# Sigmoid attention and a two-layer gated network in one kernel: the second layer's matmuls regrouped by Strassen's seven products

## The chip, the cores and the metric

The kernel runs on one core of a Trainium2 chip. The metric is device time in microseconds (us), the median of several runs: 406.16 us before (406.05 to 406.28 in 3 runs). The engines are PE (TensorE, matmuls; PEld is its weight loading), DVE (VectorE), ACT (ScalarE), POOL (GpSimd) and SP (SyncE). Each runs its own queue of instructions in order; semaphores tie them together. Matmuls write to PSUM, eight banks of 512 float32 columns on 128 partitions; everything else lies in SBUF.

## The reference

```python
scores = scale * np.matmul(q, k.transpose(0, 1, 3, 2)) - np.log(S)
attn = 1.0 / (1.0 + np.exp(-scores))
attn_out = np.matmul(attn, v)              # (8, 12, 448, 64)
x = attn_out.transpose(0, 2, 1, 3).reshape(8 * 448, 12 * 64)
h = x @ w_in                               # (3584, 768) @ (768, 2048)
g = h * (1.0 / (1.0 + np.exp(-beta * h)))
out = g @ w_out                            # (3584, 2048) @ (2048, 768)
```

Inputs and output are float32. The kernel computes its matmuls in float16 with float32 accumulation.

## The kernel before, in words

**Attention.** Eight batches of 12 heads are handled as 24 quads (a quad g is four heads; three quads make a batch b). POOL's queue loads q, k and v and casts them to float16. DVE transposes q and k (L168, L176, L180). A visit of a quad at key tile jt (0 to 3) is 8 matmuls of 32 rows (`score`, L190) into two PSUM tiles `sco` of two banks each; ACT applies the sigmoid to both (`weigh`, L201). The visit at jt = 3, the last 64 keys, takes two quads together every other time. When all four tiles of a quad are weighed, `attend` multiplies them with v (16 matmuls, L256) into two one-bank PSUM tiles, and DVE casts these to `xT` (L265), the transposed input of the dense layers for batch b.

**First layer.** `dense1(b, dc)` is one unit: six matmuls (L276) give 128 of the 2048 hidden columns for the 448 tokens of a batch in a one-bank tile; ACT takes the sigmoid with beta (L284), and DVE multiplies (L287) into `gt`, the hidden values, float16, transposed: 128 partitions x 16 chunks (dc) x 896 tokens. One gt holds a window of two batches, and there are two buffers of it.

**Second layer.** A window has seven tiles of 128 tokens. `dense2(w, t, half, part)` computes one tile's output for one half (384) of the 768 output columns: 16 matmuls (L303) over the hidden chunks, in two parts of eight. The stationary operand is the gt tile, the moving one is `w_out16`. DVE copies the result to `osb` (L316; three buffers of 768 float32 columns), and after the second half SP stores it (L334). For all batches but the last the output rows are interleaved, so a tile goes out in four stores of 32 rows; the last batch goes out with one store a tile. The very last tile is split 512 and 256.

**Order.** The order of each engine is written out by hand (`tc.manual_schedule()`). After a prologue (batch 0, in half widths, while loads come in) a loop goes over 74 visits, numbered 0 to 73 in this document. Behind each visit, units of the dense layers are taken from a list (`filler_stream`): the first layer of a batch, then the tiles that it completes. Each unit has a planned cost (M1_US 1.13, M2_US 2.6 for a half tile, so 1.3 for a part) and the quad from which it may run; a budget, `spread` for the first visits and then `rest` per visit, sets how many. An attend stands ahead of the first visit of the next quad, and DVE's transposes for the next quad behind the second and third. What the loop leaves, the `tail`, runs at the end without visits. PSUM is shared as two `sco` tiles of two banks and four one-bank buffers taken in turn by av, m1 and m2.

Of the kernel before, what the change touches and what calls it, by code (L numbers as in the profile page):

```python
# [13 lines left out]
def kernel(  # L14
# [41 lines left out]
    qTp = ctx.enter_context(tc.tile_pool(name="qTp", bufs=4))  # L56
    kTp = ctx.enter_context(tc.tile_pool(name="kTp", bufs=4))
    attnp = ctx.enter_context(tc.tile_pool(name="attnp", bufs=12))
    xTp = ctx.enter_context(tc.tile_pool(name="xTp", bufs=4))
    gtp = ctx.enter_context(tc.tile_pool(name="gtp", bufs=2))  # L60
    sigp = ctx.enter_context(tc.tile_pool(name="sigp", bufs=3))
    outp = ctx.enter_context(tc.tile_pool(name="outp", bufs=3))
    psum = {}

    def share_psum(pools: ExitStack, n_sc: int, n_one: int):
        for name, bufs in (("sc", n_sc), ("one", n_one)):
            psum[name] = pools.enter_context(
                tc.tile_pool(
                    name=f"ps_{name}{bufs}",
                    bufs=bufs,  # L70
                    space=bass.MemoryType.PSUM,
                    reuse_waits="tile",
                )
            )


    nlogs = const.tile([P, 1], FP32, name="nlogs")
# [167 lines left out]
    def attend(g: int, c0: int, n: int, part=(0, 1)):  # L245
        b, t = divmod(g, QPB)
        if b not in xTs:
            xTs[b] = xTp.tile([P, NHC, S], FP16, tag="xT", name="xT")
        slots = [2 * g + x for x in part]
        avs = [psum["one"].tile([P, S], FP32, tag="one", name="av_ps") for _ in slots]  # L250
        todo = [(s, av, jt) for s, av in zip(slots, avs) for jt in range(JF)]
        for s, av, jt in todo + [(s, av, JF) for s, av in zip(slots, avs)]:
            at = at_tiles.pop((s, jt, c0))
            base, nk = (last_base(s), KL) if jt == JF else (0, P)
            for hh in range(2):
                nc.tensor.matmul(  # L256
                    av[hh * D : (hh + 1) * D, 0:n],
                    vs[b][base : base + nk, 2 * (s % NPAIR) + hh, jt],
                    at[base : base + nk, hh, 0:n],
                    start=(jt == 0),  # L260
                    stop=(jt == JF),
                    tile_position=(base, hh * D),
                )
        for s, av in zip(slots, avs):
            nc.vector.tensor_copy(out=xTs[b][:, s % NPAIR, c0 : c0 + n], in_=av[:, 0:n])  # L265

    gts = {}
    osbs = {}

    def dense1(b: int, dc: int, c0: int = 0, n: int = S):  # L270
        w, off = b // 2, (b % 2) * S + c0
        if w not in gts:
            gts[w] = gtp.tile([P, NDC, WIN], FP16, tag="gt", name="gt")
        m1 = psum["one"].tile([P, S], FP32, tag="one", name="m1_ps")
        for hc in range(NHC):
            nc.tensor.matmul(  # L276
                m1[:, 0:n],
                w_in16[:, hc, dc * P : (dc + 1) * P],
                xTs[b][:, hc, c0 : c0 + n],
                start=(hc == 0),  # L280
                stop=(hc == NHC - 1),
            )
        sg = sigp.tile([P, S], FP32, tag="sg", name="sg")
        nc.scalar.activation(  # L284
            out=sg[:, 0:n], in_=m1[:, 0:n], func=AF.Sigmoid, bias=0.0, scale=beta_sb[:, dc : dc + 1]
        )
        nc.vector.tensor_tensor(  # L287
            out=gts[w][:, dc, off : off + n], in0=m1[:, 0:n], in1=sg[:, 0:n], op=ALU.mult
        )

    m2s = {}
    N2 = 2

    def dense2(w: int, t: int, half: int, part: int):
        gt = gts[w]
        last = w == B // 2 - 1 and t == NTILE - 1
        mid = 512 if last else HALF
        lo, hi = (0, mid) if half == 0 else (mid, DM)
        if part == 0:
            m2s[w, t, half] = psum["one"].tile([P, hi - lo], FP32, tag="one", name="m2_ps")  # L300
        m2 = m2s[w, t, half]
        for dc in range(part * NDC // N2, (part + 1) * NDC // N2):
            nc.tensor.matmul(  # L303
                m2,
                gt[:, dc, t * P : (t + 1) * P],
                w_out16[:, dc, lo:hi],
                start=(dc == 0),
                stop=(dc == NDC - 1),
            )
        if part < N2 - 1:  # L310
            return
        m2s.pop((w, t, half))
        if half == 0:
            osbs[w, t] = outp.tile([P, DM], FP32, tag="osb", name="osb")
        osb = osbs[w, t]
        nc.vector.tensor_copy(out=osb[:, lo:hi], in_=m2)  # L316
        if last:
            store(w, t, lo, hi)
        elif half == 1:
            store(w, t, 0, DM)  # L320

    def store(w: int, t: int, lo: int, hi: int):
        osb = osbs[w, t]
        c, end = t * P, (t + 1) * P
        while c < end:
            b = 2 * w + c // S
            rows, i = out[b * S : (b + 1) * S, lo:hi], c % S
            if b == B - 1:
                n = min(end - c, S - i)
                to = rows[i : i + n]  # L330
# [5 lines left out]

    M1_US, M1H_US, M2_US = 1.13, 0.58, 2.6

    def tiles_after(b: int):
        return range(0, S // P) if b % 2 == 0 else range(S // P, NTILE)  # L340

    def filler_stream():
        for c0 in (0, QH):
            for dc in range(NDC):
                if c0 and dc == 10:
                    for part in range(N2):
                        yield M2_US / N2, 0, lambda part=part: dense2(0, 0, 0, part)
                yield M1H_US, 0, lambda dc=dc, c0=c0: dense1(0, dc, c0, QH)
        for b in range(B):
            if b > 0:  # L350
                for dc in range(NDC):
                    yield M1_US, QPB * (b + 1), lambda b=b, dc=dc: dense1(b, dc)
            todo = [(t, half) for t in tiles_after(b) for half in range(2)]
            for t, half in sorted(todo, key=lambda x: x[1])[1:] if b == 0 else todo:
                for part in range(N2):
                    yield M2_US / N2, 0, lambda a=(b // 2, t, half, part): dense2(*a)

    fill = list(filler_stream())
    at_fill = [0]
# [9 lines left out]
    with tc.manual_schedule():  # L369
# [6 lines left out]
        still = const.tile([P, 512], FP16, name="still")  # L376
        nc.vector.memset(still, 0.0)  # L377
        nc.vector.memset(beta_in, 0.0)
        idle = psum["one"].tile([P, 512], FP32, tag="one", name="idle_ps")

        def idle_units(n: int):
            for _ in range(n):
# [58 lines left out]
        for g in range(QPB + 1, NQUAD, 2):  # L441
            visits += [(g, jt, ()) for jt in range(JF)] + [(g, JF, (g + 1,))]
            visits += [(g + 1, jt, ()) for jt in range(JF)]
        spread = [3 * M1H_US] * 2 + [M2_US, 6 * M1H_US] + [5 * M2_US / 7] * 7

        total = sum(u[0] for u in fill[at_fill[0] :])
        tail = 16 * M1_US + 10 * M2_US
        rest = (total - sum(spread) - tail) / (len(visits) - len(spread))
        budget, spent = 0.0, 0.0
        for i, (g, jt, also) in enumerate(visits):  # L450
            if jt == 0:
                if g > QPB:
                    attend(g - 1, 0, S)
                if g + 2 < NQUAD:
                    if g + 2 not in raws:
# [3 lines left out]
            visit(g, jt, also)  # L459
            if jt in (1, 2) and QPB < g < NQUAD - 1:  # L460
                transpose(g + 1, jt - 1)
            budget += spread[i] if i < len(spread) else rest
            if (g, jt) == (QPB, JF):
                fill_units(3)
# [41 lines left out]
```

## Time and profile before

| | |
|---|---|
| median of 3 runs | 406.16 us |
| the profiled execution | 405.89 us |
| its span, first to last instruction | 404.1 us |
| PE busy | 397.1 us, 98% |
| ACT busy | 236.9 us, 59% |
| DVE busy | 170.1 us, 42% |
| POOL busy | 77.2 us, 19% |
| granted TensorE clock | 1.000 |
| second-layer matmuls (L303) | 896 |
| first-layer matmuls (L276) | 864 |

Times of groups are sums over their instructions; "mean ns of one" counts a matmul from its start to its modelled end, so matmuls in a row overlap, and their pace is read from the time of a run of them. In a group's row the last field is how long the engine had sat idle in front of its instructions, and which engine's work ended that. In the timeline each line is the start, the duration, the engine, the line of the kernel, and the operation with its output and inputs; neighbouring ones are merged ("x8"). The program's PSUM tiles m1_ps and m2_ps appear as m_ps.

### The profile page before, as it was taken

To read this page: it belongs to the slowest core of one execution; us is meant where nothing else is said; L and a number is where in the kernel's file an instruction comes from. 1 tells how busy PE (TensorE), PEld (TensorE's weight loads), DVE (VectorE), ACT (ScalarE), POOL (GpSimd) and SP (SyncE) were. 2 spreads that over 40 slices of the span, in tenths; PEclk is the share of its full clock that TensorE was granted. 3 is DMA by queue.
4 is the path that set the end of the run, shared out by engine and by line. 5 is a ranking of instruction groups with operands and counts; after the bars stand their busy time and mean duration, and the time that the engine had idled before them with its cause. 6 is when DMAs were issued, how large, how long until landed. Compare 5 with 4: busy or idle time off the path is not lost.

```text
span 404.1 us, 7433 instructions
## 1 busy us (share of the span) xinstructions
PE 397.1 (98%) x3087; PEld 200.7 (50%) x3087; DVE 170.1 (42%) x335; ACT 236.9 (59%) x317; POOL 77.2 (19%) x133
## 2 busy tenths in 40 slices
PE   8999999999999999999999999999999999999996
PEld 3467654444554445544455444544445544555563
DVE  2446352355323563354432554245542365225421
ACT  4887856697445784387553786467834677505400
POOL 7833444410141110510114101411100000000000
PEclk9999999999999999999999999999999999999999
DMA  8999999990469212681339302492042200111022
GB/s 120 162 190 203 174 182 202 198 128 5 86 105 136 48 25 56 110 110 34 47 71 170 70 17 47 82 160 47 3 84 50 68 2 0 41 44 36 0 79 78
DMA packets 48801, 35.09 MB, mean 87 GB/s; under 512 B 28272, under 2 KB 45184, under 8 KB 48768
## 3 DMA queue, kind: packets, MB, share of 16 engines
q0 software_dynamic: 43376, 23.60, 44.9%
q1 hardware_dynamic: 5392, 11.02, 9.8%
q8 instruction: 24, 0.39, 0.4%
q14 instruction: 9, 0.07, 0.1%
HBM read 47.19 MB, written 11.01 MB: 144 GB/s over the span
## 4 chain that ended last, share of the span: by engine, by line
PE 88%; DMA 6%; POOL 3%; ACT 2%; issue 0%; DVE 0%; POOLq 0%
PE m_ps L303 36%; PE m_ps L276 35%; PE sco L190 9%; PE av_ps L256 8%; DMA w_in<-in_moe_w_in_dram 4%; ACT attnT L201 2%; DMA v<-in_v_dram 2%; POOL w_in L138 1%; POOL raw L96 1%; POOL v L117 0%; ACT sg L284 0%; DVE osb L316 0%; POOL nlogs L372 0%; POOL dummy L373 0%; POOLq L490 0%
## 5 line engine op out<-in xcount | busy, mean ns | idle before, releaser
L201 ACT ACTIVATE attnT<-sco,nlogs 128x896 f16<-128x896 f32 (+1 forms) x171 | 160.5, 992 | 104.6 <-PE sco L190 104.1
L276 PE MATMUL m_ps<-xT,w_in 128*128 128x448 f16 (+1 forms) x864 | 154.1, 332 | 0.9 <-DMA w_in<-in_moe_w_in_dram 0.7
L303 PE MATMUL m_ps<-w_out,gt 128*128 128x384 f16 (+2 forms) x896 | 153.0, 326 | 0.0
L303 PEld LDWEIGHTS <-gt 128*128 128x128 f16 x896 | 84.5, 98 | 68.0 <-issue 14.8
L287 DVE TENSOR_TENSOR gt<-m_ps,sg 128x448 f16<-128x448 f32 (+1 forms) x144 | 79.9, 572 | 87.4 <-ACT sg L284 87.3
L276 PEld LDWEIGHTS <-w_in 128*128 128x128 f16 x864 | 80.6, 98 | 71.4 <-issue 14.4
L284 ACT ACTIVATE sg<-m_ps,beta_sb 128x448 f32<-128x448 f32 (+1 forms) x144 | 82.4, 596 | 38.1 <-PE m_ps L276 36.4
L316 DVE COPY osb<-m_ps 128x384 f32<-128x384 f32 (+2 forms) x56 | 31.2, 558 | 106.2 <-PE m_ps L303 98.8
L190 PE MATMUL sco<-qT,kT 32*128 32x448 f16 (+3 forms) x864 | 53.0, 340 | 1.4 <-ACT attnT L201 0.8
L96 POOL DMA_DIRECT2D raw<-in_q_dram x27 | 14.9, 553 | 178.6 <-DVE kT L180 175.3
L256 PE MATMUL av_ps<-attnT,v 128*64 128x448 f16 (+3 forms) x432 | 42.2, 340 | 0.3 <-DMA v<-in_v_dram 0.3
L265 DVE CAST xT<-av_ps 128x448 f16<-128x448 f32 (+1 forms) x54 | 28.7, 567 | 30.5 <-PE av_ps L256 30.5
L256 PEld LDWEIGHTS <-v 128*64 128x64 f16 (+1 forms) x432 | 19.0, 107 | 24.8 <-issue 17.6
L190 PEld LDWEIGHTS <-kT 32*128 32x128 f16 (+1 forms) x864 | 13.7, 96 | 30.0 <-issue 27.6
L129 POOL DMA_DIRECT2D v<-in_v_dram x32 | 19.6, 623 | 23.4 <-DMA w_out<-in_moe_w_out_dram 13.4
L117 POOL DMA_DIRECT2D v<-in_v_dram x32 | 19.9, 640 | 7.8 <-DMA w_in<-in_moe_w_in_dram 5.2
L168 DVE STREAM_TRANSPOSE qT<-raw 128x448 f32<-128x448 f32 (+1 forms) x27 | 16.4, 614 | 3.3 <-DMA raw<-in_q_dram 3.3
L176 DVE STREAM_TRANSPOSE kT<-raw 128x384 f32<-128x384 f32 x24 | 13.6, 567 | 2.9 <-DMA raw<-in_k_dram 2.9
L96 POOL DMA_DIRECT2D raw<-in_k_dram x24 | 13.2, 549 | 1.6 <-DMA w_in<-in_moe_w_in_dram 1.6
L383 PE MATMUL idle_ps<-still 128*128 128x512 f16 x31 | 9.5, 451 | 1.2 <-DVE still L377 1.2
L138 POOL DMA_DIRECT2D w_in<-in_moe_w_in_dram x8 | 6.6, 853 | 0.3 <-DMA v<-in_v_dram 0.3
L383 PEld LDWEIGHTS <-still 128*128 128x128 f16 x31 | 3.0, 112 | 5.6 <-issue 3.2
(13 smaller groups left out, 11.8 us busy)
## 6 DMA issues: line engine op xcount, KB each, us to landing
out_dram<-osb SPq DMA_DIRECT2D x98, 96.0 KB, 1.9
raw<-in_k_dram POOLq DMA_DIRECT2D x24, 224.0 KB, 4.9
raw<-in_q_dram POOLq DMA_DIRECT2D x21, 224.0 KB, 3.6
v<-in_v_dram POOLq DMA_DIRECT2D x32, 144.0 KB, 6.9
w_in<-in_moe_w_in_dram POOLq DMA_DIRECT2D x8, 384.0 KB, 11.6
w_out<-in_moe_w_out_dram POOLq DMA_DIRECT2D x4, 768.0 KB, 15.2
v<-in_v_dram POOLq DMA_DIRECT2D x32, 48.0 KB, 5.9
out_dram<-osb SPq DMA_DIRECT2D x2, 384.0 KB, 2.3
```

The source lines that it names most:

```text
L96: nc.gpsimd.dma_start(out=raws[g][:, r, c0:c1].rearrange("p c d -> p (c d)"), in_=(q, k)[r][b, HQ * t : HQ * (t + 1)].rearrange("h (p c) d ...
L117: nc.gpsimd.dma_start(out=vs[b][i * BLK : (i + 1) * BLK, :, 0:JF].rearrange("p h j d -> p h (j d)"), in_=rows[:, :, JF * i * D : JF * (i + ...
L129: nc.gpsimd.dma_start(out=vs[b][lo : lo + BLK, :, JF], in_=rows[:, :, c])
L190: nc.tensor.matmul(sco[base : base + nk, hh, u0 : u0 + n], kT[g][lo : lo + BLK, jt * P : jt * P + nk, e], qT[g][lo : lo + BLK, c0 : c0 + n ...
L201: nc.scalar.activation(out=at[:, :, 0:n], in_=sco[:, :, 0:n], func=AF.Sigmoid, bias=nlogs[:, 0:1], scale=MSCALE,)
L256: nc.tensor.matmul(av[hh * D : (hh + 1) * D, 0:n], vs[b][base : base + nk, 2 * (s % NPAIR) + hh, jt], at[base : base + nk, hh, 0:n], start ...
L265: nc.vector.tensor_copy(out=xTs[b][:, s % NPAIR, c0 : c0 + n], in_=av[:, 0:n])
L276: nc.tensor.matmul(m1[:, 0:n], w_in16[:, hc, dc * P : (dc + 1) * P], xTs[b][:, hc, c0 : c0 + n], start=(hc == 0), stop=(hc == NHC - 1),)
L284: nc.scalar.activation(out=sg[:, 0:n], in_=m1[:, 0:n], func=AF.Sigmoid, bias=0.0, scale=beta_sb[:, dc : dc + 1])
L287: nc.vector.tensor_tensor(out=gts[w][:, dc, off : off + n], in0=m1[:, 0:n], in1=sg[:, 0:n], op=ALU.mult)
L303: nc.tensor.matmul(m2, gt[:, dc, t * P : (t + 1) * P], w_out16[:, dc, lo:hi], start=(dc == 0), stop=(dc == NDC - 1),)
L316: nc.vector.tensor_copy(out=osb[:, lo:hi], in_=m2)
```

## The change

24 of the 28 token tiles are now computed in 12 pairs. The hidden values of tiles t and t+1 are a 2 x 2 block matrix A: rows are the two tiles, columns the two halves of the 2048 hidden columns. `w_out16` is a 2 x 2 block matrix B: rows are halves of the hidden columns, columns the two halves of the 768 output columns. Instead of eight block products of eight matmuls each, a pair has seven. Two of them take a block of A as it is, five a sum or difference of two blocks; DVE makes these with one float16 instruction of 8 x 128 columns each (`hidden_sum`), two products ahead, into three buffers. Five sums of blocks of w_out are made once, by DVE, in ten half instructions behind visits 5 to 13 (`weight_sum`, `adds`).

The products of a pair accumulate in four one-bank PSUM tiles: r takes products 0 and 5, a takes 1, 4 and 6, s takes 2, b takes 3. In between, what r and a hold is read while they stay open, and the outputs of both tiles are put together from them: two copies by ACT and five adds or subtractions by DVE per pair, in place of four DVE copies. The store of tile t+1 follows product 5, that of tile t product 6.

A tile may now hold its bank across other work, so the four banks are taken by hand (`bank`): the one longest unused that is not held. If more than two are held ahead of an attend, which needs two, the loop first takes units until they aren't.

`gt` has one buffer instead of two, `xT` three instead of four. Tiles 0, 1, 2 and 27 go as before. Units of the second layer are four matmuls instead of eight, planned at 0.65 us. The planner spends 2.95 us on each of visits 11 to 31 and `rest` after them; its tail is planned at nine half tiles instead of ten.

```diff
-    xTp = ctx.enter_context(tc.tile_pool(name="xTp", bufs=4))
-    gtp = ctx.enter_context(tc.tile_pool(name="gtp", bufs=2))
+    xTp = ctx.enter_context(tc.tile_pool(name="xTp", bufs=3))
+    sump = ctx.enter_context(tc.tile_pool(name="sump", bufs=3))
...
+    def bank(name: str, cols: int = S, hold=None):
+        i = min((i for i in used if i not in held.values()), key=used.get)
+        used[i] = max(used.values()) + 1
+        if hold is not None:
+            held[hold] = i
+        return psum["one"].tile([P, cols], FP32, tag=f"one{i}", name=name)
...
-        avs = [psum["one"].tile([P, S], FP32, tag="one", name="av_ps") for _ in slots]
+        avs = [bank("av_ps") for _ in slots]
...
+    gt = const.tile([P, NDC, WIN], FP16, name="gt")
...
+    ND = NDC // 2
+    B11, B12, B21, B22 = (
+        w_out16[:, r * ND : (r + 1) * ND, c * HALF : (c + 1) * HALF]
+        for r in range(2)
+        for c in range(2)
+    )
+    ws = {
+        name: const.tile([P, ND, HALF], FP16, name=f"w_{name}")
+        for name in ("T1", "T3", "T4", "T6", "T7")
+    }
+
+    def weight_sum(name: str, part: int):
+        x, y, op = {
+            "T1": (B11, B22, ALU.add),
+            "T3": (B12, B22, ALU.subtract),
+            "T4": (B21, B11, ALU.subtract),
+            "T6": (B11, B12, ALU.add),
+            "T7": (B21, B22, ALU.add),
+        }[name]
+        rows = slice(part * ND // 2, (part + 1) * ND // 2)
+        nc.vector.tensor_tensor(out=ws[name][:, rows], in0=x[:, rows], in1=y[:, rows], op=op)
+
+    def hid(t: int, half: int):
+        return gt[:, half * ND : (half + 1) * ND, cols(t)]
+
+    def product(t: int, i: int):
+        A11, A12, A21, A22 = hid(t, 0), hid(t, 1), hid(t + 1, 0), hid(t + 1, 1)
+        return (
+            ("r", A11, None, None, ws["T3"]),
+            ("a", A22, None, None, ws["T4"]),
+            ("s", A11, A12, ALU.add, B22),
+            ("b", A21, A22, ALU.add, B11),
+            ("a", A11, A22, ALU.add, ws["T1"]),
+            ("r", A21, A11, ALU.subtract, ws["T6"]),
+            ("a", A12, A22, ALU.subtract, ws["T7"]),
+        )[i]
+
+    def hidden_sum(t: int, i: int):
+        _, x, y, op, _ = product(t, i)
+        if op is not None:
+            sums[t, i] = sump.tile([P, ND, P], FP16, tag="sum", name="sum")
+            nc.vector.tensor_tensor(out=sums[t, i], in0=x, in1=y, op=op)
+
+    def strassen(t: int, i: int, part: int):
+        name, x, _, op, w = product(t, i)
+        if part == 0 and i + 2 < NPROD:
+            hidden_sum(t, i + 2)
+        first = (t, name) not in m2s
+        if first:
+            m2s[t, name] = bank("m2_ps", HALF, (t, name))
+        m2 = m2s[t, name]
+        for dc in range(part * ND // 2, (part + 1) * ND // 2):
+            nc.tensor.matmul(
+                m2,
+                (x if op is None else sums[t, i])[:, dc],
+                w[:, dc],
+                start=first and dc == 0,
+                stop=(dc == ND - 1),
+                skip_group_check=i >= 4,
+            )
+            first = False if dc else first
+        if part == 0:
+            return
+        if i == 0:
+            for u in (t, t + 1):
+                osbs[u] = outp.tile([P, DM], FP32, tag="osb", name="osb")
...
+        if i == 1:
+            nc.scalar.copy(out=o2[:, L], in_=a)
+        elif i == 2:
+            nc.scalar.copy(out=o1[:, L], in_=m2)
+            add(o1[:, R], r, o1[:, L])
+            release((t, "s"))
+        elif i == 3:
+            add(o2[:, L], m2, o2[:, L])
+            release((t, "b"))
+        elif i == 4:
+            add(o2[:, R], a, o2[:, L], ALU.subtract)
+        elif i == 5:
+            add(o2[:, R], r, o2[:, R])
+            release((t, "r"))
+            store(t + 1, 0, DM)
+        elif i == 6:
+            add(o1[:, L], a, o1[:, L], ALU.subtract)
+            release((t, "a"))
+            store(t, 0, DM)
...
+    def second_layer(tiles):
+        for t in tiles:
+            if t < 3 or t == NT - 1:
+                for half in range(2):
+                    for part in range(N2):
+                        yield M2_US / N2, lambda a=(t, half, part): dense2(*a)
+            elif t % 2:
+                for i in range(NPROD):
+                    for part in range(2):
+                        yield M2_US / 4, lambda a=(t, i, part): strassen(*a)
...
+        for b in range(1, B):
+            for dc in range(NDC):
+                yield M1_US, QPB * (b + 1), lambda b=b, dc=dc: dense1(b, dc)
+            ends = [((x * S // P) - 1) // 2 * 2 + 1 for x in (b, b + 1)]
+            for cost, unit in second_layer(range(ends[0], NT if b == B - 1 else ends[1])):
+                yield cost, 0, unit
...
+        spread += [2.95] * (sum(g < 4 * QPB for g, _, _ in visits) - len(spread))
...
-        tail = 16 * M1_US + 10 * M2_US
+        tail = 16 * M1_US + 9 * M2_US
...
+        adds = {
+            5: [("T4", 0)],
+            6: [("T4", 1)],
+            8: [("T3", 0)],
+            9: [("T3", 1), ("T1", 0)],
+            10: [("T1", 1), ("T6", 0)],
+            11: [("T6", 1)],
+            12: [("T7", 0)],
+            13: [("T7", 1)],
+        }
...
             if jt == 0:
                 if g > QPB:
+                    while len(held) > 2:
+                        spent += fill[at_fill[0]][0]
+                        fill_units(1)
                     attend(g - 1, 0, S)
...
+            for name, part in adds.get(i, ()):
+                weight_sum(name, part)
```

A pair is named below by its first tile: pairs 3, 5, 7, ... 25. Where two pairs follow each other with no first-layer units between them, these are 3 and 5, 9 and 11, 13 and 15, 17 and 19, and 23 and 25; pairs 23 and 25 and tile 27 are in the tail.

## The prediction

> **What bounds the kernel now.** I first read the page's busy times, then the chain that ended last.
>
> ```profile
> PE 397.1 (98%) x3087; PEld 200.7 (50%) x3087; DVE 170.1 (42%) x335; ACT 236.9 (59%) x317; POOL 77.2 (19%) x133
> ...
> PE m_ps L303 36%; PE m_ps L276 35%; PE sco L190 9%; PE av_ps L256 8%; DMA w_in<-in_moe_w_in_dram 4%; ACT attnT L201 2%; DMA v<-in_v_dram 2%; POOL w_in L138 1%; POOL raw L96 1%; POOL v L117 0%; ACT sg L284 0%; DVE osb L316 0%; POOL nlogs L372 0%; POOL dummy L373 0%; POOLq L490 0%
> ```
>
> TensorE (PE) is the bound. The sums over stretches of 20 us show it busy for 20.00 in every stretch from 80 us to 380 us, so a removed matmul is time saved, and each new wait of PE is time lost, unless it falls in the load phase before 45 us. ScalarE (ACT) and VectorE (DVE) are behind it on the mean, so I next read their forms and an ordinary step of the loop.
>
> ```profile
> L303 PE MATMUL m_ps<-w_out,gt 128*128 128x384 f16 x864 | 147.8, 326 | 0.0
> ...
> L284 ACT ACTIVATE sg<-m_ps,beta_sb 128x448 f32<-128x448 f32 x112 | 69.1, 636 | 34.4 <-PE m_ps L276 34.4
> L287 DVE TENSOR_TENSOR gt<-m_ps,sg 128x448 f16<-128x448 f32 x112 | 68.1, 624 | 74.0 <-ACT sg L284 74.0
> ...
> L284 ACT ACTIVATE sg<-m_ps,beta_sb 128x224 f32<-128x224 f32 x32 | 13.4, 455 | 3.7 <-PE m_ps L276 1.9 <-DVE gt L287 0.4
> ...
> L287 DVE TENSOR_TENSOR gt<-m_ps,sg 128x224 f16<-128x224 f32 x32 | 11.8, 388 | 13.5 <-ACT sg L284 13.4
> ...
> L377 DVE MEMSET still<- 128x256 uint32 x1 | 0.3, 272 | 0.9 <-PEq L490 0.9
> ```
>
> The 326 ns of one matmul overlaps its neighbours; its pace is read from the end of the chain, where 128 of them run alone:
>
> ```profile
> 362.04 18.16 PE m_ps L276 x96
> 380.20 20.81 PE m_ps L303 x128
> ```
>
> 20.81/128 = 0.163 us each; eight are 1.30. A dense1 unit is 18.16/16 = 1.13. The timeline of one step:
>
> ```profile
> 261.30 1.64 PE L256 MATMUL av_ps<-attnT,v 128*64 128x448 f16 x16
> ...
> 262.87 0.57 PE L190 MATMUL sco<-qT,kT 32*128 32x448 f16 x8
> 262.97 1.16 DVE L265 CAST xT<-av_ps 128x448 f16<-128x448 f32 x2 [2.31 <-PE av_ps L256]
> ...
> 263.38 4.07 PE L303 MATMUL m_ps<-w_out,gt 128*128 128x384 f16 x24
> 263.48 1.91 ACT L201 ACTIVATE attnT<-sco,nlogs 128x896 f16<-128x896 f32 x2 [2.87 <-PE sco L190]
> ```
>
> An attend takes PE 1.57 (261.30 to 262.87), a visit's scores 0.51, its two weighings take ACT 1.91, the two casts that free an attend's PSUM banks take DVE 1.16, each hand-over about 0.1. ACT had idled 2.87 us before this weighing, so it has slack in the second layer's stretches.
>
> **What goes.** 24 of 28 tiles had 32 matmuls each, 768. Twelve pairs have 7 x 8 = 56, 672. The 96 that go are 96 x 0.163 = **15.6 us**. Nothing else on PE changes in number.
>
> **What comes.** ACT gets 24 copies of 384 columns: on the line through the two forms of L284, (636-455)/224 = 0.81 ns a column, 455 + 160 x 0.81 = 0.58 us, 14 us in all; ACT goes to 251 of some 390. DVE gets 60 adds with a PSUM input; by L287's forms, 1.05 ns a column, 388 + 160 x 1.05 = 0.56 us, for 48 evictions gone that took 0.56 too (L316's group): +6.7 us. It gets 60 sums of hidden tiles (1024 f16 columns) and ten half weight sums (1536). No row shows a two-input f16 sum in SBUF. L287's line carried on gives 152 + 1024 x 1.05 = 1.23 us and 1.77; that is the upper end. The only all-f16 write in SBUF, the memset of 512 f16, is done as 256 words in 272 ns; if the sum also goes by words, it is 152 + 512 x 1.05 = 0.69 and 0.96, the lower end. I take 0.69, since the two-input rows all read float32 from PSUM, which the sums don't. DVE is then 170 + 6.7 + 41 + 10 = 228 of 390 (with 1.23: 268). On the mean both are covered by idle DVE time.
>
> The Trainium skill ("VectorE: DVE Perf Modes", the perf-mode tier table) has a bf16 tensor_tensor in SBUF at two elements a cycle, 1224 ns for 2048; by its figures I estimate 0.69 for 1024, the case I took. Against the change it says ("SBUF — State Buffer", Who interferes with whom) that a VectorE instruction with two SBUF inputs contends with GpSimd's reads. In the trace before, every two-input instruction of VectorE reads one input from PSUM, so it shows nothing of this; by the rule POOL could lose at most the 51 us of sums, an estimate, and it is idle for 81% of the span.
>
> **Where PE waits anew.** Adding up the planner's costs, I numbered the 74 visits (0 to 73) and the units behind each; a pair spreads over some 2.9 visits. "3.4" is product 4 of pair 3. Four one-bank accumulators serve everything. A pair holds r over products 0 to 5, a over 1 to 6, s over 2 and b over 3, so an attend inside a pair needs the banks of s and b back. s is read by an ACT copy, b by a DVE add, and both queues are in order.
>
> Pairs that follow at once (3 to 5, 9 to 11, 13 to 15, 17 to 19; 23 to 25 in the tail) have one more link: three output buffers, two a pair, so the second pair's tile t+1 takes the buffer of the first pair's tile t. With T the end of the first pair's last product, its add ends at T+0.7. The stores:
>
> ```profile
> L334 SPq DMA_DIRECT2D out_dram<-osb x103: 314/421/1235, 66.5 to 401.5; - x103
> ...
> DMA to landing us min/median/max: 1.7/2.0/6.7
> ```
>
> Four stores of 32 rows go out 0.42 us apart; tile t+1's hold SP until T+1.1, t's go out to T+2.8 and land at T+4.8. The ACT copy of a, ready at T+2.7, stands in ACT's queue until T+4.8, and behind it stands the next visit's weighing.
>
> - Visits 20 to 22: after 3.6 come 5.0, 5.1, scores, 5.2, 5.3, then an attend at T+5.7. ACT: copy of a to T+5.4, weighing to T+7.3, copy of s to T+7.9. So the attend's first bank comes at T+8.0 (2.3 late). Then DVE: add of s 0.56, a hidden sum 0.69, add of b 0.56, to T+10.0. The second bank should have come 0.55 after the first, and comes 1.5 later still. **3.9 us** with hand-overs.
> - Visits 53 and 64 (pairs 15 and 19): the attend comes right behind product 2, at T+4.4; copies of a and s run from T+4.8 to T+6.0; the second accumulator, due T+4.95, waits 1.2; the next product then needs the bank of the first cast, 0.6 + 0.1 after the attend, with scores of 0.5 between: 0.25. **2.9 us** for both.
> - Visits 39 and 50: the same without the store, copy of s 0.7 after product 2, due 0.55: 0.2 + 0.25 each; visit 18: 0.25. **1.15 us.** At visits 29 to 32, 41 to 43, 60 and 71 banks and copies are in time.
> - Weight sums stand in visits 5 to 13 on DVE. Visits 9 and 10 get two each, 1.92 of a step of 2.45 us, with 0.42 of eviction and 0.7 of transposes: 0.6 too much each, and the casts of visit 11, which dense1 needs at once, come later. Ends 0 and 4 (at 1.77); I take **1.0**.
> - Tail: the last multiply of dense1 ends 1.5 behind PE's switch in the trace, so the first sum is ready at 2.2 us and due at 2.6. DVE needs 5 x 0.69 + 5 x 0.56 = 6.3 of a pair's 9.1. Its stores are one per tile, 3.0 behind T, and the copy delayed by them is wanted at T+5.2. **0**, with 1.23 a sum about 1 per pair.
> - One gt and three xT buffers cost nothing: every matmul that reads the old gt columns stands on PE ahead of the dense1 that overwrites them, and an xT is rewritten three batches later. If not, DVE's multiply, then the m1 banks, would be late.
> - Units of four move where a visit stands by at most 0.65 us, no work. Visits with two dense1 units instead of three give PE 0.5 + 2.27 = 2.8 for ACT's 1.91 + 1.27 = 3.2; they alternate with longer ones, so 0.
>
> **Sum.** 404.1 - 15.6 + 3.9 + 2.9 + 1.15 + 1.0 = 397.45 us of span. The profiled execution took 405.89, 1.79 more than its span, and the median is 0.27 above that: 397.45 + 2.06 = **399.5**.
>
> **Rivals.**
> 1. *The waits are covered.* If stores land sooner or ACT is ahead, the crossings cost next to nothing. For: at 254 us four issues start within 1.3 us, and ACT idles 2.87 per step. Against: the in-order queues above. 404.1 - 15.6 + 1.5 + 2.06 = 392.1.
> 2. *VectorE becomes the bound inside the pairs; slower.* At 1.23 a sum, a pair asks 6.15 + 2.8 + 0.8 attends x 1.16 + 0.8 x 1.41 of transposes = 11.0 of DVE, where PE takes 9.1 + 2.9 x 0.51 + 0.8 x 1.57 = 11.8. The add of s waits for a copy that stands behind a weighing, 1.91 + 0.58 = 2.5 of forced idling: 13.5, so +1.7 for ten pairs, 1 for each of two in the tail, 4 at the weight sums: 23 us. 404.1 - 15.6 + 23 + 2.06 = 413.6. It decides from about 0.9 us a sum (8.9 + 2.5 = 11.8 from 5 sums of 0.8 to 0.9 on), and it is slower than before once a pair loses more than 1.5. Against: the f16 memset by words.
> 3. *The copies reload ACT's table.* The one table load of the trace takes 1283 ns. Two at each of 24 copies are 61.6 us of ACT; a pair leaves ACT about 11.8 - 2.9 x 1.91 - 1.2 = 5.1, as much as is needed, but weighings and banks come 2.6 later each time. About 3 us a pair: 399.5 + 30 = 430. For it the trace shows nothing: before, the engine runs one function only.
>
> That the matmuls don't fall in number can't be: the loops count them.
>
> **Chances.** Forecast (395 to 404) 0.56, the first rival 0.26, the second 0.14, the third 0.04. The range reaches down to the first rival with its waits at nothing, 404.1 - 15.6 + 1 + 2.06 = 391.5, and up to 406, the forecast with the weight sums at 4 and the longer sums in the tail (404.5) and a further 1.5 for a store landing later. A measurement of this kernel tells some 0.2% from no change, 0.8 us. Faster 0.83 (both first cases and a little of the second), same 0.04, slower 0.13.
>
> **What would show it.** PE matmuls 2991 and busy some 15 less than before; the sum rows near 0.69 us; PE idle in front of the attends' av_ps, released by ACT copies or DVE adds, above all in visits 21 and 22 (some 130 us in); ACT copies of osb released by out_dram stores. Wrong: a second ACT table load, sums over 1 us, or PE full throughout (then 392).

## The result, and the profile after

The changed kernel takes **393.62 us**, the median of four runs (392.94 to 394.52), against 406.18 (406.05 to 406.28) in the same series: a ratio of 0.9692, 95% interval 0.9673 to 0.9712, or 12.6 us less. The profiled execution took 394.52, the slowest of the four, with a span of 392.7; before, 405.89 and 404.1. An execution of the same kernel profiled later took 393.03, with a span of 391.3. Single executions of one kernel differ by some 2 us: in later series the kernel before lay between 405.43 and 407.22, the changed kernel between 393.03 and 395.58.

The page of the changed kernel, busy time by engine and the chain that ended last:

```profile
PE 382.2 (97%) x2991; PEld 191.9 (49%) x2991; DVE 220.2 (56%) x417; ACT 247.3 (63%) x341; POOL 77.0 (20%) x133
...
PE m_ps L286 36%; PE m_ps L398 27%; PE av_ps L268 9%; PE sco L202 9%; DMA w_out<-in_moe_w_out_dram 4%; PE m_ps L316 3%; DMA w_in<-in_moe_w_in_dram 2%; DMA v<-in_v_dram 2%; POOL raw L108 1%; DMA out_dram<-osb 1%; DVE xT L277 1%; DVE osb L417 1%; POOL v L129 0%; ACT sg L294 0%; DVE gt L297 0%
```

TensorE is still the bound. It has 96 matmuls fewer and is busy 14.9 us less; the span is 11.4 shorter, so about 3.5 us of what was removed came back, nearly all of it as waits (below). VectorE gained 50 us of work, ScalarE 10, GpSimd none.

The operations that are new, in the view of groups by shape (busy, mean ns of one, idle time just before and what ended it):

```profile
L387 DVE TENSOR_TENSOR sum<-gt 128x1024 f16<-128x1024 f16 x60 | 39.2, 679 | 0.1
...
L417 DVE TENSOR_TENSOR osb<-m_ps,osb 128x384 f32<-128x384 f32 x60 | 33.3, 555 | 41.9 <-ACT osb L422 22.5 <-PE m_ps L398 18.5
...
L362 DVE TENSOR_TENSOR w_T<-w_out 128x1536 f16<-128x1536 f16 x10 | 9.1, 928 | 0.0
```

```profile
L422 ACT COPY osb<-m_ps 128x384 f32<-128x384 f32 x12 | 5.8, 480 | 5.8 <-PE m_ps L398 5.8
L420 ACT COPY osb<-m_ps 128x384 f32<-128x384 f32 x12 | 5.7, 478 | 16.4 <-PE m_ps L398 16.4
...
L501 ACT ACT_TABLE_LOAD x1 | 1.3, 1283 | 0.7 <-PEq L633 0.7
```

A hidden sum takes 0.68 us, half a weight sum 0.93, an add 0.56, a copy 0.48, and there is one table load, as before. None of the copies waited for a store: L420's idle time is put down to PE alone.

What PE waited for (line and what it waited for: us in all, times, longest). Before:

```profile
PE idle_ps L383 <- DVE still L377: 1.2, 1, 1.2
PE sco L190 <- ACT attnT L201: 0.8, 3, 0.3
PE m_ps L276 <- DMA w_in<-in_moe_w_in_dram: 0.7, 1, 0.7
```

and after:

```profile
PE m_ps L316 <- DMA w_out<-in_moe_w_out_dram: 1.7, 2, 1.4
PE av_ps L268 <- DVE osb L417: 1.3, 2, 0.7
PE idle_ps L510 <- DVE still L504: 1.2, 1, 1.2
PE m_ps L398 <- DVE xT L277: 1.0, 5, 0.2
PE m_ps L286 <- DVE osb L417: 0.6, 1, 0.6
PE sco L202 <- DVE kT L188: 0.6, 1, 0.6
```

All waits come to 3.5 us before and 7.1 after. Three things are to be seen. The waits in and behind the attends of visits 22, 53 and 64, forecast at 6.8 us, are 1.1: 0.69 at an accumulator (av_ps) in visit 22, and 0.2 each behind the attends of visits 53 and 64. The other half of the 1.3 at av_ps, 0.65, stands in visit 32, where none was forecast. A wait for w_out of 1.7 that wasn't forecast stands at the start of the second layer; the execution profiled later has none, and its waits come to 5.3. And the three waits of the scores for ScalarE (0.8), which the kernel had before, are gone.

The place where most was forecast is the attend in visit 22, inside pair 5, which follows pair 3 at once. The timeline of the changed kernel there (start, duration, instruction, idle time before it), ScalarE's queue first, then VectorE's, then the attend on PE:

```profile
115.86 0.48 ACT L420 COPY osb<-m_ps 128x384 f32<-128x384 f32 x1 [1.45 <-PE m_ps L398]
116.46 1.90 ACT L213 ACTIVATE attnT<-sco,nlogs 128x896 f16<-128x896 f32 x2
118.25 0.48 ACT L422 COPY osb<-m_ps 128x384 f32<-128x384 f32 x1
```

```profile
118.77 0.56 DVE L417 TENSOR_TENSOR osb<-m_ps,osb 128x384 f32<-128x384 f32 x1 [3.14 <-ACT osb L422]
119.24 0.68 DVE L387 TENSOR_TENSOR sum<-gt 128x1024 f16<-128x1024 f16 x1
119.84 0.55 DVE L417 TENSOR_TENSOR osb<-m_ps,osb 128x384 f32<-128x384 f32 x1
```

```profile
119.00 0.76 PE L268 MATMUL av_ps<-attnT,v 128*64 128x448 f16 x6
120.44 1.07 PE L268 MATMUL av_ps<-attnT,v 128*64 128x448 f16 x10 [0.69 <-DVE osb L417]
```

Pair 3 ended (T) at 113.2. The copy of a, forecast to wait for a store until T+4.8, ran at T+2.7, as soon as product 1 was done. The attend's first accumulator was in time; the second came 0.69 late, behind the copy of s (which stood behind a weighing), the add of s, a hidden sum and the add of b.

### The profile page after: what moved, and what is told of

The parts are those of the page before. It is cut to its first block, busy times and chain, and to the rows that moved or that the text cites. A ratio compares the mean times of both kernels' runs of the same rounds, so it can differ in the third digit from the quotient of the medians.

```text
span 392.7 us, 7403 instructions
## 1 busy us (share of the span) xinstructions
PE 382.2 (97%) x2991; PEld 191.9 (49%) x2991; DVE 220.2 (56%) x417; ACT 247.3 (63%) x341; POOL 77.0 (20%) x133
## 4 chain that ended last, share of the span: by engine, by line
PE 84%; DMA 9%; DVE 2%; POOL 2%; issue 1%; ACT 1%; SPq 0%; POOLq 0%
PE m_ps L286 36%; PE m_ps L398 27%; PE av_ps L268 9%; PE sco L202 9%; DMA w_out<-in_moe_w_out_dram 4%; PE m_ps L316 3%; DMA w_in<-in_moe_w_in_dram 2%; DMA v<-in_v_dram 2%; POOL raw L108 1%; DMA out_dram<-osb 1%; DVE xT L277 1%; DVE osb L417 1%; POOL v L129 0%; ACT sg L294 0%; DVE gt L297 0%
## 5 line engine op out<-in xcount | busy, mean ns | idle before, releaser
L398 PEld LDWEIGHTS <-sum 128*128 128x128 f16 x480 | 45.5, 98 | 37.6 <-issue 9.0
L417 DVE TENSOR_TENSOR osb<-m_ps,osb 128x384 f32<-128x384 f32 x60 | 33.3, 555 | 41.9 <-ACT osb L422 22.5
L202 PE MATMUL sco<-qT,kT 32*128 32x448 f16 (+3 forms) x864 | 51.9, 340 | 0.9 <-DVE kT L188 0.6
L398 PE MATMUL m_ps<-w_T,sum 128*128 128x384 f16 x288 | 50.5, 327 | 0.0
L108 POOL DMA_DIRECT2D raw<-in_q_dram x27 | 14.9, 552 | 169.7 <-DVE kT L192 167.0
L387 DVE TENSOR_TENSOR sum<-gt 128x1024 f16<-128x1024 f16 x60 | 39.2, 679 | 0.1
L398 PE MATMUL m_ps<-w_out,sum 128*128 128x384 f16 x192 | 34.2, 326 | 1.0 <-DVE xT L277 1.0
L398 PE MATMUL m_ps<-w_T,gt 128*128 128x384 f16 x192 | 33.7, 327 | 0.0
L398 PEld LDWEIGHTS <-gt 128*128 128x128 f16 x192 | 18.1, 98 | 14.6 <-issue 3.1
L316 PE MATMUL m_ps<-w_out,gt 128*128 128x384 f16 (+2 forms) x128 | 22.7, 327 | 1.7 <-DMA w_out<-in_moe_w_out_dram 1.7
```

What stands on the lines that cost most here:

```text
L202: nc.tensor.matmul(sco[base : base + nk, hh, u0 : u0 + n], kT[g][lo : lo + BLK, jt * P : jt * P + nk, e], qT[g][lo : lo + BLK, c0 : c0 + n ...
L316: nc.tensor.matmul(m2, gt[:, dc, cols(t)], w_out16[:, dc, lo:hi], start=(dc == 0), stop=(dc == NDC - 1),)
L387: nc.vector.tensor_tensor(out=sums[t, i], in0=x, in1=y, op=op)
L398: nc.tensor.matmul(m2, (x if op is None else sums[t, i])[:, dc], w[:, dc], start=first and dc == 0, stop=(dc == ND - 1), skip_group_check= ...
L417: nc.vector.tensor_tensor(out=out, in0=in0, in1=in1, op=op)
```

## The experiments

**Theory A**, formed from that timeline: the forecast wait is a real mechanism that the changed kernel misses, because of the buffer that the pool hands out. Tile 4's store is issued ahead of tile 3's and lands first (three of its four parts after 1.8 to 1.9 us, the last after 4.2; tile 3's took 5.5 to 6.3). Tile 6, which is written first (the copy of a), gets the third buffer, long free; tile 5, written next (the copy of s), gets tile 4's. The addresses in the built program show the order: by first writing the tiles go 0, 1, 2, 4, 3, 6, 5, 8, 7 and so on, and along this row the three buffers take turns. The prediction counted the turns by tile number and so gave tile 6 tile 3's buffer. What waits remain come from the order in which banks and adds follow. **Theory B**: the buffers don't matter, since the stores are early enough anyway, and the cost is elsewhere: the sums on VectorE, or the rate of the planned fill at the start.

### The changed kernel again

> The changed kernel as it is, as the measure of the other runs on this chip. Both theories expect 393.6 (its four earlier runs lay between 392.9 and 394.5).

Measured 393.24 us (393.03 to 395.58), ratio 0.9696 [0.9676, 0.9715]. It stood beside the next three on one chip.

### Buffers in turn by tile number

```diff
-    outp = ctx.enter_context(tc.tile_pool(name="outp", bufs=3))
+    outp = ctx.enter_context(tc.tile_pool(name="outp", bufs=1))
...
-            osbs[t] = outp.tile([P, DM], FP32, tag="osb", name="osb")
+            osbs[t] = outp.tile([P, DM], FP32, tag=f"osb{t % 3}", name="osb")
...
-                osbs[u] = outp.tile([P, DM], FP32, tag="osb", name="osb")
+                osbs[u] = outp.tile([P, DM], FP32, tag=f"osb{u % 3}", name="osb")
```

> Output buffers are given to tiles in turn (tile number modulo 3), as the prediction assumed, instead of in the order in which they come free. Theory A: the prediction's chain of waits was right and only its buffer assignment was not, so tile 6 of pair 5 now waits for the store of tile 3, ACT's copy of a holds the next weighing and the copy of s, and PE idles in front of the attends in pairs 5, 15 and 19: 4 to 7 us more than the changed kernel, 398 to 401. Theory B: ACT has enough slack in these stretches to swallow a late copy: within 0.5 us of the changed kernel.

Measured **406.81 us** (405.84 to 408.61, 12 runs), ratio 1.0018 [1.0007, 1.003]: the whole gain is gone, 13.6 us, by which of three buffers a tile is given. ScalarE's waits in this kernel, PE's, and the timeline of ScalarE and PE in visits 20 to 22:

```profile
ACT osb L420 <- DMA out_dram<-osb: 22.5, 4, 9.1
```

```profile
PE av_ps L268 <- ACT osb L422: 8.4, 3, 4.8
```

```profile
121.15 0.48 ACT L420 COPY osb<-m_ps 128x384 f32<-128x384 f32 x1 [6.76 <-DMA out_dram<-osb]
121.52 1.91 ACT L213 ACTIVATE attnT<-sco,nlogs 128x896 f16<-128x896 f32 x2
123.31 0.49 ACT L422 COPY osb<-m_ps 128x384 f32<-128x384 f32 x1
```

```profile
123.85 1.33 PE L268 MATMUL av_ps<-attnT,v 128*64 128x448 f16 x6 [4.81 <-ACT osb L422]
125.51 1.85 PE L268 MATMUL av_ps<-attnT,v 128*64 128x448 f16 x10 [0.33 <-DVE osb L417]
```

It is the chain of the prediction, link by link: the copy of a held by a store, the weighing behind it, the copy of s behind that, and PE in front of the attend's bank. (Only the second bank came 0.33 late, where 1.5 was forecast.) At pairs 15 and 19 it shows again, with waits of 2.5 and 1.1. So theory A holds, and the chain is dearer than either theory had it, for two reasons. The copy waited until T+8.0 instead of T+4.8: in this stretch stores take longer to land (the last section). And PE was slower after the wait. Sums over stretches of this kernel (from:to, length; busy us and instructions of PE, weight loads, DVE, ACT, POOL; granted clock of PE; DMA share; GB/s):

```profile
119.00:125.00 6.00, 1.19 (x7) 0.67 (x7) 1.17 (x3) 2.65 (x4) 0.80 (x2) 0.88 1.31 150
125.00:130.00 5.00, 4.67 (x26) 1.56 (x24) 2.21 (x4) 1.74 (x2) 0.00 (x0) 0.50 0.01 3
130.00:135.00 5.00, 5.00 (x34) 2.56 (x33) 2.22 (x4) 1.88 (x3) 0.00 (x0) 0.96 0.29 67
```

After the wait PE ran at half the clock for about 6 us: the attend's last ten matmuls took 1.85 us and the 20 of the second layer behind them 4.52, against 1.07 and 3.42 in the changed kernel. The two reasons make up nearly all of the difference in span to the profile after, 14.1 us: PE's waits come to 16.2 us here against 7.1 (9.1 more), and PE is busy for 386.8 us with the same 2991 matmuls, against 382.2 (4.6 more).

### A released bank counts as used when it is released

```diff
-        held.pop(key)
+        used[held.pop(key)] = max(used.values()) + 1
```

> A released bank counts as used at its release instead of at its taking. Theory A: of PE's waits in the profile, the two of 0.65 us at 160.7 and 164.9 us come from handing out the bank of r or a right after its last product, while others are long free: 1.3 us less than the changed kernel, 392.3. The waits of 0.2 us for a cast and of 0.7 at 119.8 us stay. Theory B: the wait moves to the next bank in line and nothing is gained: 393.6.

Measured 391.49 us (390.88 to 391.84), ratio 0.964 [0.9628, 0.9653]. A second series gave 392.03, ratio 0.9654 [0.9637, 0.9671]:

> The run with the banks alone once more, as the measure of the other two on this chip: 391.5 by both theories (390.9 to 391.8 before).

What it undoes is seen on PE in the changed kernel's timeline at visit 32:

```profile
157.91 2.76 PE L398 MATMUL m_ps<-w_T,sum 128*128 128x384 f16 x16
161.32 1.64 PE L268 MATMUL av_ps<-attnT,v 128*64 128x448 f16 x16 [0.65 <-DVE osb L417]
162.89 0.57 PE L202 MATMUL sco<-qT,kT 32*128 32x448 f16 x8
163.40 1.47 PE L398 MATMUL m_ps<-w_T,sum 128*128 128x384 f16 x8
165.52 1.67 PE L286 MATMUL m_ps<-xT,w_in 128*128 128x448 f16 x8 [0.65 <-DVE osb L417]
```

`bank` takes the bank that was *taken* longest ago. The banks of r and a were taken at products 0 and 1, so they are handed out the moment products 5 and 6 are done with them, while the closing add still reads them, and other banks have been free for longer. Both waits of 0.65 are gone with the edit. The gain is 1.8 us against the changed kernel beside it, and by the ratios of the second series, (0.9696 - 0.9654) x 406, 1.7 us; the two waits are 1.3 of it, the rest is not placed.

### The fill of the start, later

```diff
-        spread = [3 * M1H_US] * 2 + [M2_US, 6 * M1H_US] + [5 * M2_US / 7] * 7
+        spread = [3 * M1H_US] * 2 + [M2_US, 6 * M1H_US] + [M2_US / 2] * 4 + [M2_US] * 3
```

> The same units of tiles 0 to 2, but 1.3 us of them behind each of visits 4 to 7 and 2.6 behind 8 to 10 instead of 1.86 behind each. Theory A: the two waits of 1.7 us at 61 and 63 us come from the units of four reaching the second half of w_out before it has landed; spent later they go, and the short visits give back about 0.3 us three times: 0.8 us less, 392.8. Theory B: the load phase is bound by its transfers, and PE waits for something else instead: no gain or up to 1 us of loss.

Measured 394.56 us (394.34 to 394.98), ratio 0.9719 [0.9706, 0.9731]: 1.3 us longer than the changed kernel beside it, at the edge of what the runs tell apart (the two intervals overlap). The wait for w_out isn't there, but the changed kernel beside it had none either, and two small new waits came in this stretch (0.22 and 0.28). So that wait is not a fixed cost of the change, and no gain from later units shows. PE's waits come to 6.6 us against 5.3 in the changed kernel's trace beside it; what is left of the 1.3 more, beyond those two, stands in the first 23 us, ahead of anything that the edit touches.

### The change's side parts alone, in the kernel before

Units of four matmuls, one gt buffer, three xT buffers; no pairs.

```diff
-    xTp = ctx.enter_context(tc.tile_pool(name="xTp", bufs=4))
-    gtp = ctx.enter_context(tc.tile_pool(name="gtp", bufs=2))
+    xTp = ctx.enter_context(tc.tile_pool(name="xTp", bufs=3))
+    gtp = ctx.enter_context(tc.tile_pool(name="gtp", bufs=1))
...
-    N2 = 2
+    N2 = 4
```

> The kernel before with the change's side parts alone: units of four matmuls, one gt buffer, three xT buffers; no products of Strassen. Theory A: the buffers cost nothing, since all readers of the old gt columns stand ahead on PE; the units of four remove three waits of 0.28 us for ACT and may bring up to 1.7 us of waiting for w_out: 405.3 to 407. Theory B: one gt buffer makes DVE's multiplies late: over 408.

Measured 404.39 us (403.64 to 405.08), ratio 0.9957 [0.994, 0.9973], 1.5 us less than the kernel before in that series. The three waits of the scores for ScalarE's weighings (0.8 us in the trace before) are gone, and no wait for gt or xT came. The rest of the 1.5 is not placed.

### The hidden sums made twice

```diff
+            nc.vector.tensor_tensor(out=sums[t, i], in0=x, in1=y, op=op)
```

> Each of the 60 hidden sums is issued twice, 0.68 us more of DVE each, 41 in all; a pair then asks 5 x 1.36 of DVE, more than the 1.23 of the prediction's second rival. Theory A: DVE's idle time covers most, and only the adds and casts that free banks ahead of an attend come 0.7 later in some crossings: 394 to 397. Theory B, the rival: DVE bounds the pairs and each loses 1.7 us: 411 or more.

Measured 404.18 us (402.64 to 404.6), ratio 0.9947 [0.993, 0.9965]: 11 us of the gain gone, between what the two theories gave. VectorE is busy 259.6 us of 402.7, 64% on the mean, and yet PE waits for it:

```profile
PE m_ps L399 <- DVE osb L418: 4.3, 5, 1.2
PE av_ps L268 <- DVE osb L418: 3.4, 2, 2.0
```

All waits come to 13.6 us, against 5.3 in the changed kernel's later execution, and PE is busy for 385.2 us with the same matmuls, against 382.3; a stretch at half clock (last section) is part of that. Inside the pairs VectorE is close to full, as this kernel's sums over stretches show, first within pair 3 and then in a stretch of first-layer units (columns as above, VectorE third):

```profile
100.00:110.00 10.00, 9.79 (x76) 4.87 (x73) 9.25 (x17) 5.74 (x8) 1.05 (x2) 1.00 0.30 48
140.00:150.00 10.00, 10.00 (x77) 4.43 (x74) 5.25 (x10) 8.53 (x13) 1.06 (x2) 1.00 0.30 48
```

In 155 to 164 us, up to the longest wait (2.0), it was busy for 8.75 us of 9. So the sums are hidden at their price of 0.68 us, not at 1.36. The idle 36% lies mostly outside the pairs, where it can't help a sum that stands between a bank's last product and the add that frees it. In kind this is the bound of theory B; its cost was put too high.

### The hidden sums left out

The five sums of a pair are not made; the product reads the first block in place of the sum.

```diff
-            sums[t, i] = sump.tile([P, ND, P], FP16, tag="sum", name="sum")
-            nc.vector.tensor_tensor(out=sums[t, i], in0=x, in1=y, op=op)
+            sums[t, i] = x
```

> The 60 hidden sums are left out: a product takes the first of its two blocks as it is, so the output isn't the reference's; matmuls, adds, copies and weight sums stay. Theory A: the sums are covered but for the one between the two adds of pair 5, which holds the attend 0.7 us: 392.4 to 393.2. Theory B: sums delay casts and adds at many crossings: under 391.

Measured 392.92 us (392.41 to 394.43), ratio 0.9688 [0.9667, 0.9709]. Without any sum the kernel is not measurably faster than the changed kernel (393.24). Of PE's waits at DVE's adds only that in pair 5 is gone (0.7 us).

### Copies on VectorE

Both copies of a pair move from ScalarE to VectorE.

```diff
-            nc.scalar.copy(out=o2[:, L], in_=a)
+            nc.vector.tensor_copy(out=o2[:, L], in_=a)
...
-            nc.scalar.copy(out=o1[:, L], in_=m2)
+            nc.vector.tensor_copy(out=o1[:, L], in_=m2)
```

> The two copies of a pair run on DVE instead of ACT. Theory A: the wait of 0.7 us in pair 5 comes from the copy of s standing behind a weighing in ACT's queue; on DVE it goes, and 13 us more of DVE are covered: 392.5 to 393.2. Theory B: DVE's own queue, now with copies between sums, frees the banks of s and b later at the other crossings: 394 to 396.

Measured 393.47 us (392.99 to 393.8), ratio 0.969 [0.9675, 0.9704]: no difference. The wait in pair 5 falls from 0.68 to 0.32. With the released banks added,

> A released bank counts as used at its release, and the two copies of a pair run on DVE. Theory A: the two savings add, 0.35 us under the run with the banks alone: 391.1. Theory B: ACT was not what held the bank: 391.5.

391.53 us (391.04 to 392.93), ratio 0.9646 [0.9624, 0.9668], no different from the released banks alone.

### Sums a product earlier

The released banks, and each sum three products ahead instead of two, with a fourth sum buffer and one sigmoid buffer fewer to make room.

```diff
-    sump = ctx.enter_context(tc.tile_pool(name="sump", bufs=3))
-    sigp = ctx.enter_context(tc.tile_pool(name="sigp", bufs=3))
+    sump = ctx.enter_context(tc.tile_pool(name="sump", bufs=4))
+    sigp = ctx.enter_context(tc.tile_pool(name="sigp", bufs=2))
...
-        if part == 0 and i + 2 < NPROD:
-            hidden_sum(t, i + 2)
+        if part == 0:
+            for j in (2, 3) if i == 0 else (i + 3,):
+                if j < NPROD:
+                    hidden_sum(t, j)
```

> A released bank counts as used at its release, and the hidden sums run three products ahead (four buffers for them, paid for with one of the three sigmoid buffers). Theory A: the last bank wait of 0.7 us, in pair 5, goes, since no sum stands between the two adds any more: 0.7 us under the run with the banks alone (391.5), 390.8. Theory B: two sigmoid buffers make ACT wait for DVE in the first layer's stretches, or the third sum at a pair's start delays DVE elsewhere: 391.5 or more.

Measured 391.23 us (391.15 to 392.91), ratio 0.9647 [0.9625, 0.9669]. The wait in pair 5 stayed, 0.63: product 3 now issued the sum for product 6 exactly between the two adds, so the edit had moved one sum out of the way and another into it. With two sigmoid buffers ScalarE waits 1.6 us for VectorE in all, and the scores once for a weighing, 0.4 us. With no sum issued by product 3:

```diff
-            for j in (2, 3) if i == 0 else (i + 3,):
-                if j < NPROD:
-                    hidden_sum(t, j)
+            for j in {0: (2, 3), 1: (4,), 2: (5,), 4: (6,)}.get(i, ()):
+                hidden_sum(t, j)
```

> As the run with the banks and the sums three ahead, but product 3 issues no sum, so none stands between the adds of s and b. Theory A: the wait of 0.6 to 0.7 us ahead of the attend in pair 5 falls to 0.1 or less, and the span by 0.6; the median, 390.9 to 391.5, can hardly tell it from the run before. Theory B: the wait stays, since the copy of s behind a weighing holds the bank, not the sum.

Measured **390.65 us** (390.43 to 390.95), ratio to the kernel before 0.9613 [0.9599, 0.9627]: the fastest version found, beside 0.9692 for the changed kernel. The timeline of DVE and PE in pair 5 of this version:

```profile
117.49 1.02 DVE L418 TENSOR_TENSOR osb<-m_ps,osb 128x384 f32<-128x384 f32 x2 [2.47 <-ACT osb L423]
119.67 1.16 DVE L277 CAST xT<-av_ps 128x448 f16<-128x448 f32 x2 [1.16 <-PE av_ps L268]
```

```profile
117.78 1.85 PE L268 MATMUL av_ps<-attnT,v 128*64 128x448 f16 x16
```

The two adds follow each other, and the 16 matmuls of the attend run without a break. The wait in pair 5 is gone, as its theory A said. PE's waits come to 3.5 us, as in the kernel before, and the span is 14.9 us shorter; PE is busy 14.8 less (382.3 us against 397.1). This version ran in a series without the released banks alone beside it, so how much of the last step the removed wait brought can't be told from the medians.

## Why the prediction was right, and where it was wrong

It said 399.5 us in a range of 391.5 to 406, and faster. The direction and the range hold; the gain was put at 6.7 us and is 12.6. The stretch that it gave to its own forecast, 395 to 404, was missed: the measured time lies in the part of the range that reaches down to the first rival.

- **What goes.** 15.6 us of matmuls; PE is busy 14.9 less. Right, within 0.7.
- **What comes.** The lower end chosen for a hidden sum, 0.69, measured 0.68; half a weight sum 0.96, 0.93; an add 0.56, the same; a copy 0.58, 0.48. DVE at 220 us, put at 228. The lower end was the right choice, but the memset is weak ground for it: its row shows an instruction on 256 32-bit words, not a sum of f16 tiles, and its 272 ns are less than 152 + 256 x 1.05 = 421. From the two rows measured a sum takes (928 - 679)/512 = 0.49 ns a column. The figure in the Trainium skill ("VectorE: DVE Perf Modes", the perf-mode tier table), two elements a cycle, agrees with the 0.68 measured.
- **GpSimd's share.** Of the rule against the change ("SBUF — State Buffer", Who interferes with whom) no run here shows a cost: POOL is busy 77.0 us against 77.2, with 48 us of two-input SBUF instructions added on VectorE. POOL's rows are issues of loads and a few memsets, none with an input in SBUF, so this is hardly a test of it.
- **The waits behind stores, 6.8 us in visits 20 to 22, 53 and 64: the step that failed.** It reads "three output buffers, two a pair, so the second pair's tile t+1 takes the buffer of the first pair's tile t". The turns don't go by tile number: tile t+1 is written before tile t, so it gets the buffer that is free, and tile t the one of the first pair's tile t+1, whose store was issued first. The waits there were 0.7 and 0.4. Forcing the order that the sentence assumes brings the chain back, and costs 13.6 us; so the mechanism was right, its condition wrong, and its size also wrong, since the late landing and the clock weren't in it. Had the buffers gone by tile number, the forecast would have been too low by 7. That the measured time falls within the range is in part luck: the largest of its costs wasn't there.
- **Banks.** "At visits 29 to 32, 41 to 43, 60 and 71 banks and copies are in time" is wrong for visit 32: two waits of 0.65, from the bank chosen by the time of taking. At visits 18, 39 and 50 PE waited about 0.6 in all, put at 1.15: the 0.25 for a product that needs a bank from the casts was right (five times 0.2, those at visits 53 and 64 among them), the 0.2 for the copy of s didn't come.
- **Weight sums and tail.** Put at 1.0 and 0; measured 0 and 0.2.
- **Units of four, "no work".** Wrong by a gain: the side parts alone give 1.5 us. The three waits of scores for ScalarE stood in the waits of the kernel before, and the working didn't ask whether the shift of the visits would remove them.
- **Not forecast:** the wait for w_out, 1.7 us in one execution and 0 in the other.

Put in order for the profiled execution: 404.1 - 14.9 of matmuls and - 0.8 of the scores' waits, + 1.3 and 0.6 at the banks, + 1.0 at the casts, + 1.7 for w_out, and - 0.3 for the rest, is the 392.7 of the span.

**The rivals.** The first, waits covered, at 392.1, is nearer to the result than the forecast, but not for the reasons that it gave. Stores didn't land sooner (tile 3's took 5.5 to 6.3 us) and ScalarE wasn't ahead (in turn by tile number the chain is there); the copies never met a store, because of the buffer that they wrote to. The second, VectorE as the bound, put its point of decision at about 0.9 us a sum and 413.6 at 1.23. At a sum made twice, 1.36, the kernel takes 404.2, still faster than before; a rival of that kind exists, at some half of the price given to it, and 0.68 us a sum lies below its point of decision. The third is out, with one table load.

Left open: what brings the wait for w_out in one execution and not in the next, and the part of the side parts' 1.5 us beyond the 0.8. That the slower landing near 113 to 121 us comes from the loads that run beside the stores is an inference from the trace, and was not tried.

## What to carry to other kernels

When a pool's buffers or banks stand on the path, work out which buffer each tile really gets, in the order of first writing and of release, before pricing the wait; here that assignment alone was worth the whole change. In an in-order queue ask for every new instruction what stands behind it at that moment, and how full the engine is in that stage, not only on the mean: 64% on the mean was over 90% in stretches inside the pairs, and 11 us were lost. Rank free resources by when they were released, not by when they were taken.

## What the runs showed of the hardware

In these traces the matmul clock answers to single waits. In the kernel with buffers in turn by tile number the granted clock fell to 0.50 after PE had waited 4.8 us, and stayed there for about 6 us; after the 2.5 us wait at pair 15 it was 0.50 in 268 to 270 us; after 1.1 us it stayed at 1.00, as it did after the 1.45 us for w_out at 64.8 us of the changed kernel. With the sums made twice a wait of 2.0 us was enough in the profiled execution. Sums over stretches of that kernel, columns as above:

```profile
162.00:164.00 2.00, 0.02 (x1) 0.06 (x1) 1.86 (x4) 0.00 (x0) 2.00 (x4) 1.00 0.65 99
164.00:165.00 1.00, 0.95 (x8) 0.65 (x9) 0.00 (x0) 0.00 (x0) 1.00 (x3) 0.78 1.13 179
165.00:168.00 3.00, 3.00 (x21) 0.81 (x18) 1.16 (x2) 0.53 (x1) 2.35 (x4) 0.50 1.05 111
```

Three us at half clock do the work of 1.5, so a wait of 2.0 us cost at least another 1.5 behind it. It seems not to come each time: three of the six executions of that kernel, the profiled one among them, have a mean granted clock of 0.996 and took 404.35 to 404.60 us; the other three have 1.000 and took 402.64 to 404.01 (their waits are not on record). The Trainium skill ("TensorE: Matmul & The Clock Gate", Why this matters for your kernels) tells to avoid idle gaps of PE over some 3 us; here one of 2.0 was followed by half clock, and the measurement decides.

Stores beside loads landed late. In the changed kernel, from 108 to 122 us, DMA issues (KB each, median us to landing) read:

```profile
out_dram<-osb SPq DMA_DIRECT2D x8, 96.0 KB, 4.8
v<-in_v_dram POOLq DMA_DIRECT2D x4, 144.0 KB, 7.2
```

The first three of these stores, issued before 113 us, landed after 1.8 to 1.9 us; the five issued from 113.2 us on, beside the loads of q, k and v that start at 112.8, after 4.2 to 6.3. Over the whole kernel before, the median for a store was 2.0 us.
